# Two heads' attention scores side by side on the row halves of TensorE, in a fused attention, SwiGLU and GELU kernel

## The chip, the cores and the metric

The kernel runs on one core of a Trainium2 chip. The metric is the device time of one launch in microseconds (us), as a median over runs. A profile is one more execution, recorded by the hardware profiler.

The engines in the profile are TensorE (PE, with its weight loads as PEld), VectorE (DVE), ScalarE (ACT), GpSimd (POOL), and SyncE (SP), which here only issues DMAs.

## The reference, cut to what matters

Causal attention with an additive bias from a cumulative sum, then a gated layer with SiLU, then a layer with a sigmoid GELU. Only the attention is touched by the change:

```python
batch, n_heads, seq, head_dim = (4, 8, 576, 64)
scores = scale * np.matmul(q, k.transpose(0, 1, 3, 2))     # scale = 1/8
cum = np.cumsum(np.maximum(s, 0.0), axis=-1)
bias = -(cum[:, :, :, None] - cum[:, :, None, :])
scores = np.where(causal, -1000000000.0, scores + np.minimum(bias, 0.0))
attn = softmax(scores)                                     # with 1e-09 added to the sum
out = np.matmul(attn, v)
```

Per row of the scores the term in cum of the query is a constant and falls out of the softmax, so that the kernel only adds cum of the key to each column of the scores.

## The kernel before, in words

There are 32 heads (4 batches of 8), each of 576 positions and 64 features. A head's scores are made in five units, one PSUM bank each. A unit is one or two products of 128 queries by 64 to 448 keys (only keys that the causal mask leaves): 192 and 64 columns in unit 0, then 320, 448, 288 and 288, 1600 columns in all. After each unit DVE adds the mask, finds the row maximum and moves the scores to SBUF (the "reduction", a tensor_tensor_reduce), ACT takes the exponential and sums it, POOL divides by the sum, PE transposes the blocks (15 of 128 by 128 per head) through PSUM, ACT or DVE moves these to SBUF, and PE multiplies them with V. This last product takes two heads at once, each on one half of the array's columns (`tile_position=(0, r0)`); the trace shows its instructions as 128*64.

Scores come in two kinds. Heads 0 to 13 (`QF`) are plain: one float32 product over 128 rows, of which 64 hold the features, one the sum cum (against a row of ones), and the rest zeros. A float32 product is two matmul instructions in the trace, two passes. Heads 14 to 31 are split: q and k are rounded to float32r (one pass per product), and the remainders are kept. Product A holds on 128 rows high q with high k and low q with high k; product B holds high q with low k and two rows of cum (high and low part). To bring the halves to these rows, six DMAs per head copy 64-row pieces from SBUF to SBUF (QA, KA, QB, KB), on SP's queue, and one brings the two rows of cum from a DRAM copy.

The gated layer's first chunks (six tiles of 256 tokens, "gate products", three float32r matmuls for each weight block) are mixed into the attention on PE, as soon as all heads of a batch are done and normalised. After them PE runs one long chain for the rest of the two layers. PE's banks: scores have banks 0, 1 and 5, and bank 7 too for the first eight heads.

The order on each engine is written out at build time: `op` records each operation with a cost and a due time, and a planner (`plan`) lists them by those. The tables HD, FD, WD and TA hold due times. PE starts with idle matmuls of 512 columns (`IDLE`).

The names the change touches: `setup`, `prep_f32` and `prep` (loading q and k, rounding, copies), `scores` (the products), the tables of `PRM`, and the tiles QA, QB, KA, KB, CH and CL, which go, and QH, QL, KH, KL and KC, which come.

Of the kernel before, what the change touches and what calls it, by code (L numbers as in the profile page):

```python
# [10 lines left out]
F32 = mybir.dt.float32  # L11
F32R = mybir.dt.float32r
# [13 lines left out]
    "G0": 2, "NWS": 18, "NWO": 6,  # L26
    "QF": set(range(14)),
    "TIN": [(t * 256, 256) for t in range(6)],
    "PPB": 5, "PTB": 12, "XHB": 7, "HHB": 5,
    "VIRT": 290816,  # L30
    "SLOTS": {
        "s1": ["QB0 QB1 KB0 KB1", "B11 HH4"], "s2": ["QA0 QA1 KA0 KA1", "T1 HH5"], "s3": ["QS0 QS1 KS0 KS1", "B22 HH6"],
        "s4": ["mask", "wb"], "s5": ["SQ SQT", "SG0 SG1 V1"], "s6": ["PA0", "w9 HH0"], "s7": ["PA1", "w10 HH1"], "s8": ["PA2", "w11 HH2"],
        "si": ["PA3", "w12 HH3"], "s9": ["VS0 VS1", "M50 M51 ws"], "sb": ["PT8 PT9 PT10 PT11", "w17 HH7"], "sj": ["RE2"], "sk": ["PA4", "w6 w8"], "sl": ["w7"],
        "sc": ["SR ZR", "XH0 XH1 XH2 XH3 XH4 XH5 XH6", "MK0 MK1", "T4 w15 w16"], "sd": ["CH CL", "FH0 FH1 FH2 FH3 FH4", "B21 w13"],
        "se": ["TH0 TH1 YO", "RE0 RE1"], "sf": ["PT0 PT1 PT2", "T2"], "sg": ["PT3 PT4 PT5", "T3"], "sh": ["PT6 PT7", "w14"],
# [5 lines left out]
           (2, (8, 9)), (1, (8, 9)), (0, (8, 9)), (0, (10, 11)), (1, (10, 11)), (2, (10, 11))],  # L42
    "HD": [670.77, 588.34, 73.32, 458.6, 475.65, 350.07, 348.25, 166.97, 662.46, 625.73, 332.76, 668.93, 675.31, 193.33, 235.56, 182.94],
    "FD": [(345.51, 238.7), (69.98, 668.25), (157.32, 491.46), (669.89, 325.47), (576.97, 170.35), (699.43, 534.64)],
    "WD": [305.24, 350.84, 668.02, 164.56, 585.28, 462.76],
    "TA": 696.46, "REB": 3, "EARLY": False, "MAG": "AV", "PASS": 0, "ISSUE": 0.6, "IDLE": 7, "PEN": {}, "PVC": (0.86, 2.25),
}
# [3 lines left out]
def attention_then_swiglu_then_gelu(ctx: ExitStack, tc, qT, kT, vp, s, w1, w2, gT, out):  # L51
# [8 lines left out]
    G0 = PRM["G0"]  # L60
    QF = PRM["QF"]
    TIN = PRM["TIN"]
# [19 lines left out]
    y_d = dram.tile([P, KT, NT], F32, tag="y_d", name="y_d")  # L82
    c_d = dram.tile([HB, S], F32, tag="c_d", name="c_d")
    ch_d = dram.tile([HB, 2, S], F32, tag="ch_d", name="ch_d")
    pc_d = {
# [10 lines left out]
    wa, wm = own("wa", [512]), own("wm", [512])  # L96
    small = own("small", [128])
    small_at = [0]

    def few(n):  # L100
# [4 lines left out]
    inv_f, g_sb = few(2), few(KT)  # L105
    MX, SU, RC = [few(6) for _ in range(NB)], [few(5) for _ in range(NB)], [few(5) for _ in range(NB)]
    RY = [few(5) for _ in range(2)]

    SHAPE = {
        "Q": [S], "K": [S], "mask": [S], "SQ": [S], "VS": [5, 2 * D], "SR": [S], "ZR": [S], "CH": [S], "CL": [S], "PA": [1920], "PT": [512],  # L110
        "XH": [2, TS], "TH": [TS], "FH": [2, TS], "YO": [2, TS], "w": [2, 512], "wb": [512], "ws": [512],
        "MK": [2, 2, H2], "HH": [2, H2], "M5": [H2], "SG": [H2], "V1": [H2], "RE": [H2], **{nm: [2, 2, H2] for nm in NAMES},
    }
    ROUND = ("CH", "CL", "QA", "QB", "KA", "KB", "XH", "FH", "w", "HH", *NAMES)

# [48 lines left out]

    QS, KS, QB, KB, QA, KA, VS, TH = (get(x, 2) for x in ("QS", "KS", "QB", "KB", "QA", "KA", "VS", "TH"))
    mask, SQ, SQT, YO = (get(x) for x in ("mask", "SQ", "SQT", "YO"))
# [141 lines left out]
    def op(eng, fn, cost=None, r=None, w=None, due=None, chain=False, dma=False, g=None, after=()):  # L308
# [10 lines left out]
        if w is None:  # L319
            for name, kw in rec.calls:  # L320
                for k, x in kw.items():
                    if isap(x):
                        (wr if k in OUTS else rd).update(cells(x))
                if dma:
                    n = size(kw["out"])
                    for x in kw["out"].shape:
                        n *= x
                    o["byts"] += n
        else:
            for x in w:  # L330
                wr.update(cells(x))
            for x in r or ():
                rd.update(cells(x))
# [108 lines left out]
    def setup():  # L442
# [3 lines left out]
        op("V", lambda e: e.memset(PA[2][:, 0:512], 1.0))  # L446
        for _ in range(PRM["IDLE"]):
            op("T", lambda e: e.matmul(PB[6], PA[2][:, 0:P], PA[2][:, 0:512], start=True, stop=True), due=0.0)
        for i in range(2):
            op("G", lambda e, i=i: e.memset(KS[i][64:P, :], 0.0))  # L450
            op("G", lambda e, i=i: e.memset(QS[i][64:P, :], 1.0))
        sraw, zero, ch, cl = (get(x)[0:HB, :] for x in ("SR", "ZR", "CH", "CL"))
        cum = SQ[0:HB, :]
        dma(sraw, s)
        for h in range(2):
            prep_f32(h)
        op("V", lambda e: e.memset(zero, 0.0))
        op("V", lambda e: e.tensor_scalar(out=sraw, in0=sraw, scalar1=0.0, scalar2=8.0, op0=ALU.max, op1=ALU.mult))
        op("V", lambda e: e.tensor_tensor_scan(out=cum, data0=zero, data1=sraw, initial=0.0, op0=ALU.add, op1=ALU.add))
        for h in range(2):  # L460
            dma(KS[h][64:65, :], SQ[h:h + 1, :], eng="A", cost=0.6)
        dma(c_d, cum, eng="A", cost=0.6)
        for i in range(NB):
            op("G", lambda e, i=i: e.memset(SU[i], 1.0))
        for t in PA:
# [7 lines left out]
           cost=0.3)  # L473
        op("G", lambda e: make_identity(nc, ident), cost=0.5, w=[ident])
        rnd("V", ch, cum, cost=0.74)
        dma(ch_d[:, 0, :], ch.bitcast(F32))
        sub(cl, cum, ch, eng="V")
        dma(ch_d[:, 1, :], cl.bitcast(F32))
        for i in range(2):
            op("G", lambda e, i=i: e.memset(QB[i][64:P, :].bitcast(F32), 1.0))  # L480
            op("G", lambda e, i=i: e.memset(KB[i][64:P, :].bitcast(F32), 0.0))
        for i in range(2):
            op("V", lambda e, i=i: e.memset(VS[i][64:P, 4, :], 0.0))
        dma(g_sb, gT)

    def prep_f32(h):
        b_, hh = divmod(h, H)
        dma(QS[h % 2][0:64, :], qT[b_, hh])
        dma(KS[h % 2][0:64, :], kT[b_, hh])
        if h > 1:  # L490
            dma(KS[h % 2][64:65, :], c_d[h:h + 1, :])

    def prep(h):
        b_, hh = divmod(h, H)
        i = h % 2
        if h % 2 == 0:
            v = VS[h // 2 % 2]
            dma(v[:, 0:4, :], vp[b_, hh // 2, 0:4 * P, :].rearrange("(k p) d -> p k d", p=P))
            dma(v[0:64, 4, :], vp[b_, hh // 2, 4 * P:S, :])
        if h in QF:  # L500
            if h > 1:
                prep_f32(h)
        else:
            if i == 0:
                for t, part, src in ((QS[0], QS[1], qT), (KS[0], KS[1], kT)):
                    dma(t, src[b_, hh:hh + 2].rearrange("h d s -> (h d) s"))
                    rnd(PRM["RQ"], part.bitcast(F32R), t)
                    sub(t.bitcast(F32R), t, part)
            r0 = 64 * i
            (ql, qh), (kl, kh) = ([t[r0:r0 + 64, :] for t in x] for x in (QS, KS))  # L510
            for t, c0, x in ((QA, 0, qh), (KA, 0, kh), (KA, 64, kh), (QA, 64, ql), (QB, 0, qh), (KB, 0, kl)):
                dma(t[i][c0:c0 + 64, :].bitcast(F32), x)
            dma(KB[i][64:66, :].bitcast(F32), ch_d[h])

# [5 lines left out]
    def scores(h, u):  # L520
        ps = bank(h, "s", 5 * h + u)
        blks = {0: [(1, 0, 0, 192), (0, 192, 0, 64)], 1: [(2, 0, 0, 320)], 2: [(3, 0, 0, 448)],
                3: [(4, 0, 0, 288)], 4: [(4, 0, 288, 288)]}[u]
        i = h % 2

        def fn(e):
            for qb, c0, k0, n in blks:
                q0 = Q0[qb]
                o = ps[:, c0:c0 + n]
                if h in QF:  # L530
                    e.matmul(o, QS[i][:, q0:q0 + P], KS[i][:, k0:k0 + n], start=True, stop=True)
                else:
                    e.matmul(o, QA[i][:, q0:q0 + P], KA[i][:, k0:k0 + n], start=True, stop=False)
                    e.matmul(o, QB[i][:, q0:q0 + P], KB[i][:, k0:k0 + n], start=False, stop=True)

        first_score.append(op("T", fn)["i"])
        mx = MX[h % NB]
# [238 lines left out]
    for h in range(HB):  # L776
        prep(h)
        for u in range(5):
            scores(h, u)
        if h == 0:  # L780
            first_weights()
        recip(h)
        for qb in range(5):
            norm(h, qb)
        for t in range(4):
            transp(h, t)
        b_, hh = divmod(h, H)
        if hh % 2:
            for piece in range(2):
                pv(h - 1, piece, PRM["HD"][h // 2])  # L790
        if hh % 2:
            rms_sq(b_, hh // 2)
        if hh == H - 1:
            rms(b_)
            for j, (t0, n) in enumerate(TIN):
                if (t0 + n - 1) // S == b_:
                    fa_tile(j, fill_due)
# [322 lines left out]
    n = 0  # L1120
# [335 lines left out]
```

## Time and profile before

| what | value |
|---|---|
| median of 3 runs | 1005.71 us (1004.41 to 1006.68) |
| the profiled execution | 1005.69 us, its span 1003.9 us |
| PE busy | 991.6 us, 99% of the span |
| DVE, ACT, POOL busy | 65%, 56%, 28% |
| granted TensorE clock | 1.000 of full speed |

The attention with the gate products mixed in lasts from the start to about 262 us; from there PE runs the long chain of the two layers, which the change does not touch. PE's busy share is made of matmuls whose ends are modelled and overlap, so for PE the start times say more: the start of one group of matmuls to the start of the next is what the group took from PE's time. A row of the timeline groups neighbours by the first one's shape, so "128x192 x4" may hold two matmuls of 192 columns and two of 64.

### The profile page before, as it was taken

Reading aid. Unit: us, or ns where it says so; the run is one execution under the profiler, and the core shown is the slowest. Engines: PE = TensorE matmul, PEld = TensorE weight load, DVE = VectorE, ACT = ScalarE, POOL = GpSimd, SP = SyncE. Lnnn points to the kernel's source line nnn. Section 1 sums busy time; section 2 is a strip of 40 time slices with the busy share of each in tenths; the row PEclk is TensorE's granted clock in tenths of the full one; section 3 lists DMA queues with packets and bytes.
Section 4 is the critical chain, followed back from the end, with each engine's and each line's share of the span. In section 5 each row is a group of like instructions: output and inputs, shape, how many; then the busy total and the mean of one; then the engine's idle time right before and its main releaser. Section 6 shows DMA issues by size and latency. Waiting matters only on the chain. (4 is left out here: it accounts for less than half of the span.)

```text
span 1003.9 us, 16588 instructions
## 1 busy us (share of the span) xinstructions
PE 991.6 (99%) x5890; PEld 912.1 (91%) x5890; DVE 654.1 (65%) x1528; ACT 559.6 (56%) x1290; POOL 281.8 (28%) x387
## 2 busy tenths in 40 slices
PE   8999989999999999999999999999999999999998
PEld 5778878988899999999999999999889998899987
DVE  6788776767978887545866858874653565353323
ACT  6888976767676555334444436775644463353322
POOL 6665653443333223002321303232320231020000
PEclk9999999999999999999999999999999999999999
DMA  4436885762776763661484576653275045405541
GB/s 143 129 117 171 224 220 158 182 167 61 275 250 245 279 255 100 247 219 43 143 320 166 215 287 242 276 196 138 91 297 220 23 154 241 191 1 193 203 170 63
DMA packets 63186, 183.61 MB, mean 183 GB/s; under 512 B 7120, under 2 KB 24016, under 8 KB 63104
## 3 DMA queue, kind: packets, MB, share of 16 engines
q1 hardware_dynamic: 62992, 182.49, 53.1%
q8 instruction: 46, 0.75, 0.3%
q14 instruction: 36, 0.29, 0.1%
q10 hardware_dynamic: 112, 0.08, 0.0%
HBM read 122.35 MB, written 44.26 MB: 166 GB/s over the span
## 5 line engine op out<-in xcount | busy, mean ns | idle before, releaser
L205 ACT ACTIVATE s<-b 128x384 f32<-128x384 f32 (+1 forms) x267 | 127.7, 489 | 144.6 <-PE b L205 79.5
L205 DVE TENSOR_TENSOR xT<-b,xT 128x384 f32<-128x384 f32 (+1 forms) x158 | 92.5, 599 | 88.7 <-PE b L205 87.0
L205 ACT ACTIVATE b<-b 128x384 f32<-128x384 f32 x125 | 58.2, 478 | 107.6 <-DVE b L205 71.8
L205 PE MATMUL b<-s 128*128 128x288 f32 (+6 forms) x476 | 113.1, 367 | 3.4 <-DMA s<-s 1.7
L205 POOL TENSOR_TENSOR wa<-wa,st 128x512 int32<-128x512 int32 x50 | 65.3, 1306 | 178.2 <-DVE wa L205 83.7
L205 DVE TENSOR_TENSOR s<-b,s 128x384 fp32r<-128x384 f32 (+1 forms) x121 | 66.4, 554 | 69.5 <-ACT s L205 65.2
L205 PE MATMUL b<-s,w 128*128 128x384 f32 x540 | 107.0, 335 | 0.4 <-DVE s L205 0.2
L205 PEld LDWEIGHTS b<-s,w 128*128 128x128 f32 x540 | 94.9, 188 | 1.5 <-DVE s L205 1.0
L205 PEld LDWEIGHTS b<-s 128*128 128x128 f32 x476 | 75.5, 191 | 17.9 <-issue 6.6
L205 DVE TENSOR_TENSOR b<-b,s 128x384 f32<-128x384 f32 x82 | 46.1, 563 | 51.3 <-PE b L205 42.8
L205 POOL TENSOR_SCALAR wm<-wm 128x512 f32<-128x512 f32 x68 | 41.8, 615 | 120.2 <-ACT wm L205 42.2
L205 PE MATMUL b<-sc,w 128*128 128x256 f32 (+1 forms) x396 | 68.0, 305 | 0.0
L205 ACT ACTIVATE s<-s,small 128x448 f32<-128x448 f32 (+4 forms) x100 | 55.2, 554 | 21.3 <-DVE small L205 20.7
L205 POOL TENSOR_SCALAR s<-s,small 128x576 f32<-128x576 f32 (+4 forms) x100 | 52.1, 540 | 27.7 <-PE b L205 14.6
L205 PE MATMUL b<-sd,w 128*128 128x384 f32 (+1 forms) x312 | 58.3, 315 | 0.8 <-ACT se L205 0.8
L205 PEld LDWEIGHTS b<-sc,w 128*128 128x128 f32 x396 | 57.2, 190 | 1.6 <-issue 0.5
L205 ACT ACTIVATE st<-st 128x512 int32<-128x512 uint32 x68 | 45.6, 671 | 19.3 <-DMA st<-in_w_dram 19.3
L205 PE MATMUL b<-s,s 128*128 128x384 f32 (+1 forms) x252 | 54.9, 346 | 0.0
L205 PE MATMUL b<-w,s 128*128 128x512 f32 x189 | 51.1, 391 | 0.0
L205 PE MATMUL b<-s,sk 128*128 128x384 f32 x246 | 50.8, 335 | 0.0
L205 PEld LDWEIGHTS b<-sd,w 128*128 128x128 f32 x312 | 49.3, 189 | 1.2 <-ACT se L205 1.0
L205 PE MATMUL b<-s,sc 128*128 128x384 f32 x228 | 47.2, 334 | 0.0
(261 smaller groups left out, 2348.8 us busy)
## 6 DMA issues: line engine op xcount, KB each, us to landing
st<-in_w_dram SPq DMA_DIRECT2D x68, 512.0 KB, 3.5
s<-s SPq DMA_DIRECT2D x108, 144.0 KB, 2.7
xT<-y_d SPq DMA_DIRECT2D x3, 1536.0 KB, 7.9
s<-pc11B SPq DMA_DIRECT2D x6, 768.0 KB
s<-pc21B SPq DMA_DIRECT2D x6, 768.0 KB, 6.6
out_dram<-xT SPq DMA_DIRECT2D x18, 256.0 KB, 2.4
s<-in_vp_dram SPq DMA_DIRECT2D x16, 256.0 KB, 3.2
y_d<-se SPq DMA_DIRECT2D x12, 256.0 KB, 3.3
```

The source lines that it names most:

```text
L205: return lambda *args, **kw: f(*[real(x) for x in args], **{k: real(x) for k, x in kw.items()})
```

## The change: heads in pairs, one on each half of the rows

A unit of scores now makes both heads of a pair. Head 0 of the pair lies on rows 0 to 63, head 1 on rows 64 to 127 of the same tiles, as one DMA brings them. Each product is issued twice, once with `tile_position=(0, 0)` and once with `(64, 0)`, into two banks. Pairs 0 to 3 (`QP`) are plain: one float32 product over 64 rows. The other twelve pairs are split, as three float32r products (high by high, high by low, low by high). In both kinds one more float32r product adds cum: the constant tile KC holds high and low parts of all heads' sums on 32 rows each, and a column of zeros with two ones, broadcast to 128 columns, is the stationary operand that picks the head's two rows. No copies within SBUF are left, nor the DRAM copies of cum. q and k of a pair, which lie side by side, are rounded in one operation of 1152 columns and the remainder taken in another. The tables of due times are new, and there are six idle matmuls in place of seven.

```diff
-    "QF": set(range(14)),
+    "QP": set(range(4)),
...
-    "TA": 696.46, "REB": 3, ..., "IDLE": 7, "PEN": {}, "PVC": (0.86, 2.25),
+    "TA": 501.91, "REB": 3, ..., "INNER": 1.7, "IDLE": 6, "PEN": {}, "PVC": (1.0, 2.25), "SCC": (0.23, 0.13),
...
-        for i in range(2):
-            op("G", lambda e, i=i: e.memset(KS[i][64:P, :], 0.0))
-            op("G", lambda e, i=i: e.memset(QS[i][64:P, :], 1.0))
...
-        for h in range(2):
-            dma(KS[h][64:65, :], SQ[h:h + 1, :], eng="A", cost=0.6)
-        dma(c_d, cum, eng="A", cost=0.6)
+        rnd("AV", KC[:, 0:S], SQ)
+        for r in (HB, 3 * HB):
+            sub(KC[r:r + HB, 0:S], SQ[r:r + HB, :], KC[r:r + HB, 0:S])
+        for r, c in ((0, 0), (64, 65)):
+            x, y = (ident[r:r + 64, z:z + HB - 1:2] for z in (c, c + HB))
+            tt(KC[r:r + 64, S:S + HB // 2], x, y, ALU.add)
...
-            for t, c0, x in ((QA, 0, qh), (KA, 0, kh), (KA, 64, kh), (QA, 64, ql), (QB, 0, qh), (KB, 0, kl)):
-                dma(t[i][c0:c0 + 64, :].bitcast(F32), x)
-            dma(KB[i][64:66, :].bitcast(F32), ch_d[h])
+        if h // 2 not in QP:
+            raw, hi, lo = wide(KS[i], 2), wide(KH[i], 2).bitcast(F32R), wide(KL[i], 2).bitcast(F32R)
+            rnd(PRM["RQ"], hi, raw)
+            sub(lo, raw, hi)
...
     def scores(h, u):
-        ps = bank(h, "s", 5 * h + u)
+        i = h // 2 % 2
+        pss = [bank(h, "s", 10 * (h // 2) + 2 * u + j) for j in range(2)]
...
+        pairs = [(QS, KS)] if plain else [(QH, KH), (QH, KL), (QL, KH)]
         def fn(e):
-            for qb, c0, k0, n in blks:
-                if h in QF:
-                    e.matmul(o, QS[i][:, q0:q0 + P], KS[i][:, k0:k0 + n], start=True, stop=True)
-                else:
-                    e.matmul(o, QA[i][:, q0:q0 + P], KA[i][:, k0:k0 + n], start=True, stop=False)
-                    e.matmul(o, QB[i][:, q0:q0 + P], KB[i][:, k0:k0 + n], start=False, stop=True)
+            for x, (qt, kt) in enumerate(pairs):
+                for y, (qb, c0, k0, w) in enumerate(blks):
+                    for j, ps in enumerate(pss):
+                        r = slice(64 * j, 64 * j + 64)
+                        e.matmul(ps[:, c0:c0 + w], qt[i][r, Q0[qb]:Q0[qb] + P], kt[i][r, k0:k0 + w],
+                                 start=x == 0 and y == 0, stop=False, skip_group_check=True, tile_position=(64 * j, 0))
+            for y, (qb, c0, k0, w) in enumerate(blks):
+                for j, ps in enumerate(pss):
+                    r = slice(64 * j, 64 * j + 64)
+                    e.matmul(ps[:, c0:c0 + w], KC[r, S + h // 2:S + h // 2 + 1].to_broadcast([64, P]), KC[r, k0:k0 + w],
+                             start=False, stop=y == len(blks) - 1, skip_group_check=True, tile_position=(64 * j, 0))
```

The order of PE at the start, before the change, from the second head's unit 2 on. Banks 0, 1, 5 and 7 hold scores, s3 holds q and k, s6 and s8 hold a head's attention weights, and ident marks a transpose:

```order
L205 MATMUL b7_73<-s3_0_137 128x448
L205 MATMUL b5_71<-s3_0_137 128x320
L205 MATMUL b0_66<-s3_0_137 128x288
L205 MATMUL b1_67<-s3_0_137 128x288
L205 MATMUL b2_68<-ident_120,s6_0_184 128x128 x4
```

The same place after the change, from unit 2 of the second pair (sj is the constant tile KC):

```order
L208 MATMUL b5_71<-s3_0_135 128x448
L208 MATMUL b7_73<-s3_0_135 128x448
L208 MATMUL b5_71<-sj_0_149 128x448
L208 MATMUL b7_73<-sj_0_149 128x448
L208 MATMUL b0_66<-s3_0_135 128x288
L208 MATMUL b1_67<-s3_0_135 128x288
L208 MATMUL b0_66<-sj_0_149 128x288
L208 MATMUL b1_67<-sj_0_149 128x288
L208 MATMUL b2_68<-ident_118,s6_0_163 128x128 x4
```

Ahead of the first transposes there were ten units of one head (heads 0 and 1); now there are nine units of two heads (pair 0 and four fifths of pair 1).

In the middle, before the change, a unit of a split head (s2 and s1 hold the A and the B operands) between transposes:

```order
L205 MATMUL b3_69<-ident_120,sk_0_210 128x128 x4
L205 MATMUL b5_71<-s2_0_978 128x288
L205 MATMUL b5_71<-s1_0_216 128x288
L205 MATMUL b2_68<-ident_120,sk_0_210 128x128 x4
```

And the last unit of the last pair after the change (s2 holds the high and low parts; w marks gate products or their second layer). Between its first two rows and its last two stand two more such pairs of rows:

```order
L208 MATMUL b2_68<-ident_118,si_0_194 128x128 x4
L208 MATMUL b7_73<-sd_0_1363,w5_129 128x256 x3
L208 MATMUL b5_71<-s2_0_657 128x288
L208 MATMUL b0_66<-s2_0_657 128x288
...
L208 MATMUL b5_71<-sj_0_149 128x288
L208 MATMUL b0_66<-sj_0_149 128x288
L208 MATMUL b6_72<-sc_1_970,w0_124 128x256 x3
```

Two matmuls of one head over 128 rows have become eight of two heads over 64 rows each. What lies on either side (transposes and gate products) still runs over 128 rows and 128 columns. Over the whole order the scores form 70 stretches: 64 are entered from work on the whole array (39 from transposes, 20 from gate products, 5 from the normalisation) and 6 from a product with V; 64 are left to work on the whole array (41 to transposes, 21 to gate products, 2 to the normalisation) and 6 to a product with V.

## Rows read from the trace of the kernel before

**Rows 1.** Busy time by stretch: us, then busy (and count) of each engine, clock, DMA.

```profile
25.00:75.00 50.00, 50.00 (x353) 37.56 (x352) 39.53 (x154) 42.47 (x127) 33.55 (x55) 1.00 0.40 123
75.00:125.00 50.00, 50.00 (x406) 42.49 (x405) 40.17 (x145) 43.50 (x135) 29.29 (x48) 1.00 0.75 197
175.00:225.00 50.00, 50.00 (x426) 45.75 (x422) 36.81 (x135) 34.81 (x103) 21.00 (x39) 1.00 0.67 177
```

**Rows 2.** PE's waits in 0 to 262 us: total, times, longest.

```profile
PE b L205 <- DMA s<-s: 1.7, 1, 1.7
PE b L205 <- POOL s L205: 1.7, 1, 1.7
PE b L205 <- ACT se L205: 0.8, 1, 0.8
PE b L205 <- ACT sb L205: 0.7, 1, 0.7
```

**Rows 3.** PE's timeline, 16 to 20 us: start, us, instructions [wait before].

```profile
16.69 0.66 PE L205 MATMUL b<-ident,s 128*128 128x128 f32 x4 [1.68 <-POOL s L205]
17.18 2.97 PE L205 MATMUL b<-s 128*128 128x192 f32 x12
19.99 0.71 PE L205 MATMUL b<-ident,s 128*128 128x128 f32 x5
```

**Rows 4.** PE's timeline, split units: starts of a unit and of what follows.

```profile
172.34 0.53 PE L205 MATMUL b<-s 128*128 128x192 f32 x4
172.70 0.36 PE L205 MATMUL b<-sd,w 128*128 128x256 f32 x1
...
194.38 0.52 PE L205 MATMUL b<-sd,w 128*128 128x256 f32 x3
194.74 0.57 PE L205 MATMUL b<-s 128*128 128x448 f32 x2
195.15 0.52 PE L205 MATMUL b<-sd,w 128*128 128x256 f32 x3
195.50 0.43 PE L205 MATMUL b<-s 128*128 128x288 f32 x2
195.77 0.49 PE L205 MATMUL b<-ident,sk 128*128 128x128 f32 x3
```

**Rows 5.** PE's timeline, 31 to 34 us, around a product with V.

```profile
31.43 1.04 PE L205 MATMUL b<-ident,s 128*128 128x128 f32 x8
32.40 0.43 PE L205 MATMUL b<-sf,s 128*64 128x256 f32 x1
32.41 0.43 PE L205 MATMUL b<-sg,s 128*64 128x256 f32 x1
...
33.20 0.76 PE L205 MATMUL b<-s 128*128 128x192 f32 x4
```

**Rows 6.** PE's timeline, 41 us: one step of 320 columns to the next.

```profile
41.25 0.43 PE L205 MATMUL b<-sb,s 128*64 128x320 f32 x1
41.26 0.43 PE L205 MATMUL b<-sf,s 128*64 128x320 f32 x1
41.52 0.43 PE L205 MATMUL b<-sb,s 128*64 128x320 f32 x1
```

**Rows 7.** PE's timeline, 204 us: three transposes of 64 and 128 rows.

```profile
204.30 0.72 PE L205 MATMUL b<-ident,small 64*128 64x64 f32 x3
204.95 0.63 PE L205 MATMUL b<-sd,w 128*128 128x256 f32 x3
205.41 0.60 PE L205 MATMUL b<-ident,s 128*128 128x128 f32 x4
```

**Rows 8.** DVE groups, 0 to 262 us: reductions, and a remainder.

```profile
L205 DVE CUSTOM_DVE_ANT_0 s<-b,s 128x448 f32<-128x448 f32 (+4 forms) x100 | 39.2, 424 | 10.9 <-PE b L205 10.7
L205 DVE TENSOR_TENSOR s<-s 128x576 fp32r<-128x576 f32 x12 | 9.0, 762 | 0.7 <-ACT s L205 0.6
L205 DVE TENSOR_SCALAR s<-s 128x576 fp32r<-128x576 f32 x13 | 6.0, 465 | 0.4 <-DMA s<-ch_d 0.4
```

**Rows 9.** DMA issues of the whole run.

```profile
s<-s SPq DMA_DIRECT2D x108, 144.0 KB, 2.7
```

## What the change was predicted to do

> **What bounds the kernel now.** I read the busy shares by stretch first. In the attention PE is busy all of the time in three stretches of 50 us, where DVE has 37 to 40 us of work, ACT 35 to 44 and POOL 21 to 34 [rows 1]. The clock is granted in full in each. Next I read what PE waits for: four waits of 0.7 us or more in 262 us, 4.9 us together [rows 2]. So PE's own work sets the end of this stage; the chain after it is untouched and dense. The change is then priced by PE's time alone: what each kind of work takes from one start to the next, since ends are modelled.
>
> **Scores, now.** A plain head (12 matmuls) starts at 17.18 and the transposes behind it at 19.99: 2.81 us [rows 3]. Of this 2.67 are columns (1600, two passes, two cycles each at 2.4 GHz). Units of a split head take 0.36 (192 and 64 columns, A and B), 0.41 (448) and 0.27 (288) [rows 4]; I put 320 columns between these, at 0.30. A split head is 0.36 + 0.30 + 0.41 + 2 x 0.27 = 1.61 us. All scores: 14 x 2.81 + 18 x 1.61 = 68.3 us.
>
> **Scores, after.** No row shows two products on row halves. The nearest are the products with V, two heads on the column halves: the two start 0.01 us apart, and the next step of 320 columns comes 0.27 us later, which is the two passes of one of them [rows 6]. So two halves do run in the time of one there, their weight loads included. I take the same for row halves. A plain pair is then one head's 2.81 and one float32r product for the sums, half of 1.61: 3.6 us. A split pair is four products, 4 x 0.805 = 3.2 us, and 0.1 more in unit 0, where a step of 64 columns cannot be shorter than the weight load of 128 columns (0.10, below). In all 4 x 3.65 + 12 x 3.35 = 54.8 us, 13.5 less than before. Who looks closer sees where it comes from: the four plain pairs save 2.0 each, the three pairs that turn from plain to split 2.3 each, and the nine pairs that were split already save nothing (3.35 for 3.22): two products per head before, four per two heads now. The bounds: with no overhead beyond columns 45.3 us, 23 less than before; with the halves one after the other 110 us, 41 more.
>
> **What it adds: changes of the array's shape.** The product with V is the one kind of work that often leaves the whole array, and its rows show a price. Eight transposes (0.86 by their columns) start at 31.43 and the product only at 32.40: 0.11 lost on the way in. Its 384 columns of two passes take 0.64; the next scores start 0.80 after its start: 0.16 lost, the load of the first weights and the way out [rows 5]. That could be a matter of column halves. But three small transposes over 64, 128 and 64 rows stand in the trace, at 128 columns each way of the weights: 0.65 us for 0.21 of columns [rows 7], so each change between 64 and 128 rows costs some 0.145, a drain of 0.095 and 0.05 of load that nothing hides. And the three gate products behind them take 0.46 where three such take 0.36 elsewhere [rows 7, 4]: their first load of 128 columns is bare too, 0.10. A load of a score's operand is of that kind.
>
> So a stretch of scores on row halves pays 0.095 + 0.10 on entry, and on leaving 0.095 + 0.05 before transposes or 0.20 before gate products. The order has 64 entries from the whole array, 43 exits to transposes and the normalisation and 21 to gate products: 64 x 0.195 + 43 x 0.145 + 21 x 0.195 = 12.5 + 6.2 + 4.1 = 22.8 us. Products with V are as many as before and pay as before. The bounds: the drain alone, 128 x 0.095 = 12.2 us, if loads slip under it; nothing, if float32r products change shape freely, for which no row speaks; and no row shows more than 0.20 at a change.
>
> The Trainium skill (TensorEngine Tiling (Array Packing), Key Properties) says that a change of tiling mode drains TensorE, and names no price. The 0.095 agrees with that, and the row adds the bare load, of which the rule says nothing; by the drain alone the total of this document would be near 1002.
>
> **The rest.** Copies within SBUF go (108 of 144 KB on SP's queue [rows 9]), and with them the one PE wait on such a copy: -1.7 us [rows 2]. Behind the copies SP's queue held loads of weights, which PE never waits for by name, so no more is counted. What is late next at that place is the rounding of the pair, an operation of DVE, ACT or POOL.
>
> Rounding and remainders: twelve pairs for nine, one operation for two. By DVE's rows two of each are 2 x (0.465 + 0.762) = 2.5 us per pair of heads [rows 8], so three more pairs add at most 7.4 us over three engines. PE's work covers it; the tightest is ACT with 43.5 of 50 us [rows 1]. If all of it fell on one engine that PE waits for, it would cost those 7.4.
>
> The start: one idle matmul less is two passes of 512 columns, -0.86. But DVE now reduces both heads in turns, so head 0 is done at the eleventh reduction, not the sixth, five times 0.424 later [rows 8], and the transposes that now start at 16.69, after a wait of 1.68 for POOL [rows 3], would start at 16.69 + 2.1 - 0.86 = 17.9. PE's nine units of a pair are over at 15.3 (9.4, from 16.69 - 1.68 - 2 x 2.81, less 0.86, plus 0.2 and 9 x 0.73), so it waits 2.6: 0.9 more than now. Together zero.
>
> Banks: from the fifth pair on a unit takes two of three banks, so the next one waits on PE until the first half is reduced (0.42 us), with all of PE's queue behind it. The order puts transposes or gate products between most units: 80 units stand in 70 stretches, so ten follow one another directly, most of them in the first pairs with four banks. I count nothing; at most 10 x 0.42 = 4.2.
>
> The end of the stage: more gate products are left behind the last product with V, which covers the wait of 0.8 for ACT [rows 2]: -0.8.
>
> **Sum.** -13.5 + 22.8 - 1.7 + 0 - 0.8 = +6.8 us. On the profiled execution (1005.69, of which 1003.9 are the span), which is the median of the runs, that makes 1012.5.
>
> **Rivals.** First, faster: the halves run nearer to their columns, since one half's pauses are filled by the other, and the loads at a change slip under the drain. For it: in rows 6 a step of two halves has no more than 0.003 over its columns. Against it: those are float32 passes; a float32r unit of 288 columns takes 0.27 for 0.24 [rows 4], and the bare load is seen at every kind of work. With half of the two gaps to the bounds (-18 and +17.5) the sum is -3.0, 1002.7; with all of them -23 + 12.2 - 2.5 = -13.3, 992.4. It is at 997 in the middle.
>
> Second, the change does not do what it says: weight loads or streams of the two row halves take turns. If each step paid its load, 24 steps of a split pair and 18 of a plain one would add 12 x 2.4 + 4 x 1.8 = 36 us: 1049; if the streams themselves took turns, 1012.5 + 55 = 1067. Against it stand rows 6, where two loads and two streams share a step. The Trainium skill (TensorE: Matmul & The Clock Gate, Part 3, The mechanism) has a rule for the first: a weight load overlaps a running matmul only if its row group differs. By it half 0's next load would wait for half 0's running product, and the 1049 follow. The trace disagrees on the whole array, where all loads have the same rows: gate products keep 0.12 a piece [rows 4] though each has a load of 0.10, so I give it little.
>
> Third, slower by waits: DVE's reductions, now in pairs, set the pace, as PE needs two banks at once. It decides from the point where DVE is over 0.4 us late at a unit. DVE has 20% to spare [rows 1], and PE itself gets slower; if every second of the 60 split units waited one reduction, 30 x 0.42 = 12.7 us more, 1025.
>
> **Chances.** The forecast 0.52, faster by denser halves 0.30, loads or streams in turns 0.08, paced by DVE 0.10. A measurement of this kernel tells 0.2%, 2 us, from no change. Slower by more than that: 0.52 + 0.08 + 0.10, less some of the forecast's own lower edge, 0.64; the denser halves give 0.26 faster; 0.10 lies between. The forecast's own range is 1007 to 1019. To hold 8 in 10 the range takes in most of the denser halves (from 994) and the paced case (to 1028).
>
> **What would show it.** In the profile after: the two matmuls of a step start 0.01 apart, and a split unit of 288 columns takes some 0.54 (0.27 if it were one product per head, 1.1 if in turns). Between the last gate product or transpose and the first score 0.2 us are missing, and as much on the way out. The first transposes start near 18. The stage's end moves from 262 to about 269, and the long chain behind it keeps its 742 us. I am wrong if the changes of shape cost less than 0.1 a side, if a step stays clearly under its columns plus 0.013, or if PE has waits of over 5 us in the stage.

## The result, and the profile after

The changed kernel takes 1019.79 us (median of four runs, 1018.54 to 1020.15), the kernel before 1005.06 beside it: the ratio is 1.014, its 95% interval 1.0125 to 1.016. The forecast was 1012.5, slower by 6.8; it is slower by 14.7. So the sign and the main mechanism came out as forecast, and two further losses of about 6 us each had been put at nothing. The time lies just above the forecast's own range of 1007 to 1019, and inside the wide one of 994 to 1028.

The page of the profile after, its first lines:

```profile
span 1018.2 us, 16887 instructions
PE 1006.3 (99%) x6224; PEld 913.9 (90%) x6224; DVE 647.6 (64%) x1507; ACT 565.7 (56%) x1292; POOL 295.7 (29%) x389
PEclk8999999999999999999999999999999999999999
```

PE is as full as before, on a span 14.3 us longer. To place these I mark the two matmuls `b<-w` of 512 columns that open the long chain, and its last group of three. In PE's timeline before:

```profile
268.25 0.63 PE L205 MATMUL b<-w 128*128 128x512 f32 x2
...
999.30 0.84 PE L205 MATMUL b<-sk,s 128*128 128x512 f32 x3
```

And after:

```profile
276.52 0.62 PE L208 MATMUL b<-w 128*128 128x512 f32 x2
...
1013.67 0.85 PE L208 MATMUL b<-sk,s 128*128 128x512 f32 x3
```

The chain opens 8.27 us later, and from its opening to its last group it takes 737.15 us where it took 731.05: another 6.10, though it holds the same matmuls in the same order. (The first two expectations below count to the end of the span, 741.7 and 735.6; the later ones count to the last matmul itself, 0.46 later than here: 737.6 and 731.5.)

What answers to [rows 2] in the stage before the chain, PE's waits in 0 to 285 us:

```profile
PE b L208 <- DMA s<-in_qT_dram: 2.3, 1, 2.3
PE b L208 <- DVE small L208: 1.8, 2, 1.5
PE b L208 <- DVE sj L208: 1.1, 2, 0.8
PE b L208 <- POOL s L208: 0.7, 2, 0.4
```

These are the first four of nine kinds; all nine come to 7.9 us. The wait for a copy within SBUF is gone. New are waits for q and for the constant tile sj, both in the first 14 us. The 1.5 for `small` stands ahead of PE's first matmul; the kernel before has the like of it, 1.4, which [rows 2] leave out, so it does not enter the difference. What answers to [rows 3], PE's start:

```profile
10.64 0.80 PE L208 MATMUL b<-s 64*128 64x192 f32 x8 [2.32 <-DMA s<-in_qT_dram]
12.26 0.53 PE L208 MATMUL b<-sj 64*128 64x192 f32 x1 [0.82 <-DVE sj L208]
13.05 0.52 PE L208 MATMUL b<-sj 64*128 64x192 f32 x2 [0.26 <-DVE sj L208]
...
23.29 0.66 PE L208 MATMUL b<-ident,s 128*128 128x128 f32 x4 [0.28 <-POOL s L208]
```

The first transposes start at 23.29, where 16.69 was and near 18 was forecast. And what answers to [rows 4], the middle:

```profile
183.45 0.60 PE L208 MATMUL b<-sd,w 128*128 128x256 f32 x3
183.98 0.71 PE L208 MATMUL b<-s 64*128 64x320 f32 x6
184.52 0.31 PE L208 MATMUL b<-sj 64*128 64x320 f32 x2
184.76 0.62 PE L208 MATMUL b<-sd,w 128*128 128x256 f32 x3
```

Here one reads the price of a change of shape. Six matmuls on row halves are three steps of 320 columns, and a step within a stretch takes 0.145 us (median of all such steps): 0.44. They take 0.54, 0.10 more, which is the bare first load of the forecast. The step of the sums takes 0.24, 0.09 more than 0.145, which is the forecast's drain ahead of the gate products.

### The profile page after: what moved, and what is told of

Read it like the earlier page. It is cut to its first block, busy times and chain, and to the rows that moved or that the text cites. A ratio compares the mean times of both kernels' runs of the same rounds, so it can differ in the third digit from the quotient of the medians.

```text
span 1018.2 us, 16887 instructions
## 1 busy us (share of the span) xinstructions
PE 1006.3 (99%) x6224; PEld 913.9 (90%) x6224; DVE 647.6 (64%) x1507; ACT 565.7 (56%) x1292; POOL 295.7 (29%) x389
## 4 chain that ended last, share of the span: by engine, by line
PE 95%; DVE 3%; DMA 1%; ACT 1%; POOL 1%; issue 0%; DVEq 0%
PE b L208 95%; DMA sc<-in_s_dram 1%; DVE s L208 1%; DVE xT L208 1%; POOL s L208 1%; ACT s L208 0%; DVE sd L208 0%; DVE sj L208 0%; DVE b L208 0%; DVE sf L208 0%; ACT sf L208 0%; ACT sg L208 0%; DVE sb L208 0%; ACT L208 0%; DVE sc L208 0%
## 5 line engine op out<-in xcount | busy, mean ns | idle before, releaser
L208 PE MATMUL b<-s 64*128 64x288 f32 (+6 forms) x618 | 92.6, 360 | 4.2 <-DMA s<-in_qT_dram 2.3
L208 PEld LDWEIGHTS b<-s 64*128 64x128 f32 (+1 forms) x618 | 58.3, 190 | 21.5 <-issue 11.4
L208 PE MATMUL b<-sc,w 128*128 128x256 f32 (+1 forms) x396 | 70.1, 309 | 0.0
L208 ACT ACTIVATE s<-s,small 128x192 f32<-128x192 f32 (+4 forms) x100 | 55.1, 553 | 15.3 <-DVE small L208 14.9
L208 POOL TENSOR_SCALAR s<-s,small 128x192 f32<-128x192 f32 (+4 forms) x100 | 52.9, 549 | 20.6 <-DVE small L208 10.6
L208 DVE CUSTOM_DVE_ANT_0 s<-b,s 128x192 f32<-128x192 f32 (+4 forms) x100 | 40.1, 426 | 15.2 <-PE b L208 14.3
```

The costliest lines, as they stand in the source:

```text
L208: return lambda *args, **kw: f(*[real(x) for x in args], **{k: real(x) for k, x in kw.items()})
```

## Experiments on the long chain: where its 6.1 us come from

Neither PE's order nor that of another engine differs in the chain. What differs is where buffers stand in SBUF: the tile `small` is shorter, so that everything behind it begins 32 bytes past a multiple of 64, and buffers get their place in the order of first use, which is another one.

**A shift of everything.** In after_align `small` moves behind all buffers, which puts the rest on multiples of 64; in before_off32 the kernel before gets the shift.

```diff
+    tail = ctx.enter_context(tc.tile_pool(name="tail", bufs=1))   # after_align
...
-    small = own("small", [72])
+    small = tail.tile([P, 72], F32, tag="small", name="small")
-    small = own("small", [128])                       # before_off32
+    small = own("small", [104])
```

> The changed kernel with one edit: the small tile (288 bytes per partition) moved to the end of SBUF, so that every other tile starts at a multiple of 64 bytes again, as before the change, and not 32 bytes past one. The orders of all engines stay as in the changed kernel. Theory A (the offset makes TensorE's reads slower): the chain behind the attention, which takes 741.7 us in the profile after and 735.6 before from the same two matmuls to the end, goes back to 735.6 to 736.5; total about 1014, 5.5 to 6.5 us less. Rival (another cause, as the transfers of the chain or the clock): the chain stays at 741 to 742 and the total at 1019 to 1020.

> The kernel before the change with one edit: the small tile is 416 bytes per partition in place of 512, so that all tiles behind it start 32 bytes past a multiple of 64. Orders unchanged. Theory A: the chain behind the attention goes from 735.6 to 741 to 742 us, the total to about 1011. Rival: no difference, 1005 to 1006.

Measured: after_align 1019.74 (ratio 1.015, 1.0135 to 1.0165), its chain 737.2; before_off32 1006.49 (1.0014, 1.0004 to 1.0024), its chain 730.96. The theory fell: a shift common to all buffers behind `small` does nothing to the chain.

**The order of the buffers.** Two kernels give every buffer its first tile at the start, in the other kernel's order. Nothing moves on any engine.

```diff
+    for slot in "s8 sc s3 s9 s4 s5 sd s6 s7 si sk s1 sf sg sh sb s2 se sl sj".split():   # after_place: order of before
...
+        tiles[slot, 0] = slots.tile(...)
...
-    small = own("small", [128])                                                         # before_place: order of after
+    small = own("small", [96])
...
+    WIDE["sj"] = 2240
...
+    for slot in "s8 sc s3 s4 sj s9 s6 s7 s5 si sk sf sg sh sb s1 s2 se sd sl".split():
...
+        tiles[slot, 0] = slots.tile(...)
```

> The changed kernel, its buffers in SBUF laid out in the order of the kernel before; every engine's order is unchanged. Theory (the long chain is slower because its operands lie elsewhere relative to one another): the chain goes back from 737.6 to some 731.5, the total from 1019.8 to 1013.7. Rival (what slows the chain is not the place of its operands): chain within 1 of 737.6, total within 1.5 of 1019.8.

> The kernel before, its buffers in SBUF laid out in the order of the changed kernel; every engine's order is unchanged. Theory (place of the operands): the chain goes from 731.5 to some 737.6, the total from 1005.0 to 1011. Rival: chain within 1 of 731.5, total within 1.5 of 1005.

Measured: after_place 1014.34 (1.0101, 1.0079 to 1.0123), before_place 1012.24 (1.0076, 1.0059 to 1.0092). Two groups of the chain by shape (busy, mean ns of one), before:

```profile
L205 PE MATMUL b<-s,w 128*128 128x384 f32 x540 | 107.0, 335 | 0.4 <-DVE s L205 0.2
L205 PE MATMUL b<-w,s 128*128 128x512 f32 x189 | 51.1, 391 | 0.0
```

after:

```profile
L208 PE MATMUL b<-s,w 128*128 128x384 f32 x540 | 107.4, 337 | 0.2
L208 PE MATMUL b<-w,s 128*128 128x512 f32 x189 | 51.6, 394 | 0.0
```

after_place:

```profile
L208 PE MATMUL b<-s,w 128*128 128x384 f32 x540 | 107.2, 335 | 0.4 <-DVE s L208 0.2
L208 PE MATMUL b<-w,s 128*128 128x512 f32 x189 | 51.1, 391 | 0.0
```

before_place:

```profile
L206 PE MATMUL b<-s,w 128*128 128x384 f32 x539 | 107.4, 337 | 0.2
L206 PE MATMUL b<-w,s 128*128 128x512 f32 x189 | 51.4, 393 | 0.0
```

The loss goes and comes with the places, in both directions: the chain takes 731.91 in after_place and 736.78 in before_place. (The shorter `small` of before_place shifts all buffers behind it alike.) From one start to the next, a mean over the chain without gaps over 0.25 us, a matmul of 384 columns takes 173.7 ns in the kernel before and 174.7 in the changed one, one of 512 takes 228.3 and 231.1. That is 0.6 and 1.2%, at a granted clock of 1.00 in both, and over the chain's some 3060 and 865 matmuls 5.5 of the 6.1 us; the rest is in the longer gaps.

**Order, or an offset.** In the kernel before every buffer has a multiple of 256 bytes a row. In the changed kernel sj holds the constant tile with its 16 unit columns, 592 elements or 2368 bytes, and stands fifth: all buffers behind it are 64 bytes off, modulo 256, against those ahead. (In before_place, by its 2240 bytes, it is 192.) after_uc gives the unit columns a tile of their own (sj, now 2304 bytes, also comes three places later, by its first use); before_pad128 lengthens one buffer of the kernel before by 128 bytes.

```diff
-        ... "KC": [S + HB // 2], ...                   # after_uc
+        ... "KC": [S], ...
...
+    UC = own("uc", [HB // 2], F32R)
...
+    WIDE["s4"] += 128                                  # before_pad128
```

> The changed kernel with the unit columns in a small tile of their own, so that the constant tile's buffer has 2304 bytes a row, a multiple of 256 like all other buffers, and no longer 2368; buffers stay in the changed kernel's order, the engines' work is the same. Theory (buffers behind that one stand 64 bytes off, modulo 256, against those ahead of it, and this slows the chain): chain 731.5 to 732.5, total near 1014. Rival (the order of the buffers in SBUF is what counts): chain 737.6, total 1019.8.

> The kernel before with one buffer (mask, wb) 128 bytes a row longer, so that the buffers behind it stand 128 bytes off against those ahead, modulo 256; every engine's order is unchanged. Theory (offsets count modulo 256, so 128 costs as 64 and 192 did): chain 735 to 738 instead of 731.5, total 1009 to 1012. Rival (they count modulo 128, and 64 was the bad one): chain within 1 of 731.5, total within 1.5 of 1005.

Measured: after_uc 1014.93 (1.009, 1.0069 to 1.0111), before_pad128 1011.61 (1.0059, 1.0035 to 1.0082). Their timelines, after_uc:

```profile
276.73 0.63 PE L209 MATMUL b<-w 128*128 128x512 f32 x2
...
1008.59 0.84 PE L209 MATMUL b<-sk,s 128*128 128x512 f32 x3
```

before_pad128:

```profile
268.57 0.62 PE L206 MATMUL b<-w 128*128 128x512 f32 x2
...
1006.98 0.86 PE L206 MATMUL b<-sk,s 128*128 128x512 f32 x3
```

The chains take 731.86 and 738.41. So with the changed kernel's order otherwise kept, the 64 bytes make the loss, and 128 bytes put into the kernel before cost it 7.4 us. The order by itself costs nothing that these runs show. Offsets of 64, 128 and 192 have all been seen to cost, multiples of 256 not (in after_uc and before, buffers of 9 times 256 bytes stand in the middle). What in the memory does this stays open; I didn't find a rule that tells which pair of operands is slow.

## Experiments on the start

**s sooner, and no half clock.** In the changed kernel one DMA with repeated rows brings s, 8.3 us from issue (0.74) to landing (9.07). after_s4 takes four DMAs of 32 rows. And between 12 and 18 us the changed kernel's clock is granted at half level, behind 2.3 us in which PE waited; after_idle12 has idle matmuls until the scores begin.

```diff
-        dma(sraw, bass.AP(s.tensor, s.offset, [(0, P // HB), (S, HB), (1, S)]), due=0.0)   # after_s4
+        for r in range(0, P, HB):
+            dma(sraw[r:r + HB, :], s, due=-90.0)
...
-    ... "IDLE": 6, ...                                                                     # after_idle12
+    ... "IDLE": 12, ...
```

> The changed kernel with one edit: s is loaded by four DMAs of 32 rows each, not by one DMA that repeats it four times (which landed at 9.07 us, issued at 0.74). Theory B (the late sums hold the start): the scan starts at about 6, the first reduction at 10 to 10.5 in place of 13.74, the first transposes at about 20 in place of 23.3, total 3 to 4 us less, about 1016. Rival (the start is paced by the reductions of two heads in turns, whatever the load): the first transposes come less than 1.5 us earlier and the total stays within 1.5 us of 1019.8.

> The changed kernel with twelve idle matmuls in place of six: PE is busy until about 13.5 us, has no 2.3 us wait at the start, and should keep its full clock (in the profile after, 6.8 us at half the clock follow the wait). Scores start 3 us later. Theory C (the half clock is what the start loses): 3 us or more less, 1016 or below. Theory B (the late sums and DVE set the first transposes, the clock little): within 1.5 us of 1019.8, and the first transposes between 22.5 and 24.

Measured: after_s4 1019.36 (1.0146, 1.013 to 1.0163), first transposes at 22.28; after_idle12 1020.29 (1.016, 1.0143 to 1.0177), clock 1.00 throughout, first transposes at 23.12. Neither helps by itself, but neither settles its question. The four DMAs brought s no sooner: DVE could start on it at 8.35, and with the one DMA at 8.38 to 9.08 in five profiles. And the full clock of after_idle12 is paid for with a later start of the scores. Its first reduction and its first transposes:

```profile
14.54 0.36 DVE L208 CUSTOM_DVE_ANT_0 s<-b,s 128x192 f32<-128x192 f32 x1 [2.24 <-PE b L208]
```

```profile
23.12 0.66 PE L208 MATMUL b<-ident,s 128*128 128x128 f32 x4 [0.28 <-POOL s L208]
```

DVE's timeline in the changed kernel, from the landing of s on:

```profile
9.08 0.46 DVE L208 TENSOR_SCALAR sc<-sc 128x576 f32<-128x576 f32 x1 [6.37 <-DMA sc<-in_s_dram]
9.58 1.36 DVE L208 TENSOR_TENSOR_SCAN s<-sc 128x576 f32<-128x576 f32 x1
10.97 0.46 DVE L208 TENSOR_SCALAR sj<-s 128x576 fp32r<-128x576 f32 x1
11.46 1.53 DVE L208 TENSOR_TENSOR sj<-s,sj 32x576 fp32r<-32x576 f32 x2
13.74 0.36 DVE L208 CUSTOM_DVE_ANT_0 s<-b,s 128x192 f32<-128x192 f32 x1 [0.75 <-POOL small L208]
...
16.87 0.62 DVE L208 CUSTOM_DVE_ANT_0 s<-b,s 128x448 f32<-128x448 f32 x1 [0.95 <-PE b L208]
```

Scan, rounding and remainders take 3.9 us behind s, and only then can any unit be finished by its sums. The first reduction starts at 13.74; before it was at 10.05. From there to the first transposes it takes 9.55 us (13.74 to 23.29), where after_idle12 at full clock takes 8.58 (14.54 to 23.12): at half level DVE waits for PE, 0.95 us at 16.87 alone. So the half clock costs about 1 us here, and after_idle12 gives 0.8 of it back by its later first reduction.

**Without that path.** after_nosum makes the constant tile from zeros, and so leaves the sums out, with s by four DMAs as in after_s4 and all buffers where the changed kernel has them.

```diff
...
-        op("V", lambda e: e.tensor_tensor_scan(out=SQ, data0=zero, data1=sraw, ...))
-        rnd("AV", KC[:, 0:S], SQ)
+        rnd("AV", KC[:, 0:S], zero)
...
```

> The changed kernel with s loaded by four DMAs and the constant tile made from zeros at once, so that no score waits for the scan (the sums are left out of the scores); same buffers, same places. Theory (the start is late because the first reductions wait for qT and for the constant tile, and because both heads are reduced in turns): first reduction near 11 instead of 13.74, first transposes near 20.3 instead of 23.3, total 3 less, near 1016.8. Rival (the turns or the half clock alone hold the start): first transposes stay beyond 22, total within 1.5 of 1019.8.

Measured: 1015.0 (1.0101, 1.0075 to 1.0128). In its timelines the first reduction and the first transposes, and the opening of the chain:

```profile
9.35 0.36 DVE L208 CUSTOM_DVE_ANT_0 s<-b,s 128x192 f32<-128x192 f32 x1 [4.36 <-PE b L208]
```

```profile
17.95 0.66 PE L208 MATMUL b<-ident,s 128*128 128x128 f32 x4 [0.29 <-POOL s L208]
...
271.20 0.62 PE L208 MATMUL b<-w 128*128 128x512 f32 x2
```

The chain opens 5.3 us sooner than in the changed kernel, more than expected, and the first transposes stand where the forecast had them (17.9). From the first reduction to there it takes 8.60, against 6.64 before the change (10.05 to 16.69): 1.96 more for the 2.1 of the forecast. So the forecast had the turns of both heads right, and what it left out is the path by the constant tile, and q, which lands behind s. Of the 5.3 us, 4.4 are the earlier first reduction; 0.95 is the half clock that follows PE's waits in the changed kernel, while here the clock is granted in full throughout. Without all this the stage is still 2.95 longer than before (271.20 to 268.25).

## Experiments on the price of a change of shape

The kernel before gets one extra float32 matmul of 64 columns ahead of each of 64 groups of transposes, over 64 rows in the one and over 128 in the other.

```diff
+            if h >= 16:
+                e.matmul(ps[:, ...], ident[0:64, :], ident[0:64, 0:64], start=True, stop=True)      # before_visit64
+                e.matmul(ps[:, ...], ident[0:128, :], ident[0:128, 0:64], start=True, stop=True)    # before_visit128
...
```

> The kernel before with one added matmul of 64 columns over 64 rows ahead of each of the 64 groups of transposes of heads 16 to 31 (the output doesn't use it). Theory (leaving the whole array and coming back costs 0.195 + 0.145): 64 x 0.34 = 22 us more than the control over 128 rows, at least 18. Rival (a change of shape is cheap, the loss in the changed kernel is elsewhere): under 6 us more than the control.

> Control to the one over 64 rows: the same added matmul of 64 columns, over all 128 rows, at the same 64 places. Both theories: only its own time, two passes of some 0.06 to 0.11, 8 to 14 us over the kernel before.

Measured: 1038.04 (1.0344, 1.0293 to 1.0394) and 1015.42 (1.0106, 1.0091 to 1.0121), 22.6 us apart. Three of the four executions over 64 rows show a mean granted clock of 0.987 to 0.996, and the profiled one has the half level from 134 to 161 us; the one at full clock took 1034.28, which is 18.9 over the control, or 0.295 for each visit. The timelines, in stretches at full clock, of before_visit64:

```profile
222.23 0.42 PE L205 MATMUL b<-s 128*128 128x288 f32 x2
222.58 0.43 PE L205 MATMUL b<-ident 64*128 64x64 f32 x2
222.94 0.66 PE L205 MATMUL b<-ident,sk 128*128 128x128 f32 x4
```

and of before_visit128:

```profile
199.38 0.43 PE L205 MATMUL b<-s 128*128 128x288 f32 x2
199.65 0.33 PE L205 MATMUL b<-ident 128*128 128x64 f32 x2
199.81 0.61 PE L205 MATMUL b<-ident,sk 128*128 128x128 f32 x4
```

From the score to the transposes it is 0.71 against 0.43: 0.28 for going to 64 rows and back, with the same columns. The theory held; the price in the forecast (0.195 in, 0.145 out) was some 15% high for this kind of visit.

## A version meant to beat both

Split heads are the cheaper ones for PE, so the kernel before was given more of them.

```diff
-    "QF": set(range(14)),
+    "QF": set(range(8)),
```

> The kernel before with 8 plain heads instead of 14, so six heads more are split (float32r); its plan is made anew by the same rules. Theory (PE bounds the stage, and a split head takes 1.61 for 2.81 of a plain one): 6 x 1.2 = 7.2 us less, near 998. Rival (the copies within SBUF and the roundings that split heads need come too late early in the stage, and PE waits for them): gain under 2 us, or a loss.

Measured: 1012.28 (1.0067, 1.0041 to 1.0094), slower. PE's waits in 0 to 280 us, the longest kinds:

```profile
PE b L205 <- ACT sf L205: 1.9, 3, 1.0
PE b L205 <- DMA s<-ch_d: 1.9, 2, 1.1
PE b L205 <- POOL s L205: 1.8, 1, 1.8
PE b L205 <- POOL sk L205: 1.5, 1, 1.5
```

The rival held in that there is no gain and PE waits more: all kinds listed in that view come to 13.2 us, against 7.9 in the kernel before. But these 5.3 us do not account for everything: the chain opens 4.25 later (272.50 for 268.25), so PE's other time fell by only 1.0 and not by 7.2. Why is not shown. The due times were made for 14 plain heads, so this doesn't show that no plan with eight could win.

## Why the prediction was right, and where it was not

For the terms, each kind of matmul got its median time to the next start as its pace; what lies above it, up to 0.25 us, is counted by the kinds of the two neighbours, and longer gaps as waits. In us:

| term | forecast | measured |
|---|---|---|
| scores themselves | 68.3 to 54.8: -13.5 | 73.2 to 54.7: -18.5 |
| changes of shape, products with V apart | +22.8 | +20.3 |
| start, to the first transposes | 0 | +5.3 |
| long chain | 0 | +6.1 |
| the rest: PE's other waits, end of the stage, and what is left to the sum | -2.5 | +1.2 |
| sum | +6.8 | +14.4 |

What the forecast was about, denser scores against changes of shape and the rest, makes 3.0 us of this, 2.95 by after_nosum. So the sign was forecast for the right reason, but most of the 14.7 came by the two terms that were put at nothing, and that the time still fell near the forecast's own range is in part luck.

**Two halves side by side: right.** The two matmuls of a step start 3 to 6 ns apart, and the pace of all scores comes to 54.7 us, for 54.8 (in after_nosum, whose start does not blur it; 55.7 in the changed kernel). The rival by which loads or streams take turns (36 or 55 us more) is out: within a stretch a step of 320 columns takes 0.145 us, 0.012 over its columns, with no load showing. With it goes, here, the time that would follow from the rule of the Trainium skill (TensorE: Matmul & The Clock Gate, Part 3, The mechanism) which the prediction cites. Loads do show in unit 0, where columns are few. PE's weight loads there:

```profile
49.78 0.74 PEld L208 LDWEIGHTS b<-s 64*128 64x128 f32 x12 [0.17 <-issue]
50.44 0.30 PEld L208 LDWEIGHTS b<-sj 64*128 64x128 f32 x4
```

Twelve loads in six pairs take 0.66 us, 0.11 a pair, so that a product of 192 and 64 columns takes two such, 0.22, for 0.107 of columns. The two halves load side by side, and the 0.1 more that the forecast gave unit 0 for this was near: four products at 0.22, not at half of 0.36, make 0.16 more.

**Changes of shape: right, and the cause of the loss that was meant.** By neighbours: drains on the way in 5.4, the first step's bare load 5.3, drains on the way out 5.4, bare first loads of the transposes and gate products behind 4.1; 20.3 together. A drain is 0.09 to 0.10 each way, as [rows 7] had it.

**Scores before: the term came out larger.** I priced a split head at 1.61 from single units [rows 4]. Summed over all 18 they take 34.1, 1.90 each; the plain ones 39.1, as forecast. By this count denser work on halves was worth 5 us more than I gave it. But part of the 5 us is only a matter of which neighbour is charged. The units priced in [rows 4] stand behind gate products; the next one stands between transposes:

```profile
195.77 0.60 PE L205 MATMUL b<-ident,sk 128*128 128x128 f32 x4
196.12 0.51 PE L205 MATMUL b<-s 128*128 128x288 f32 x2
196.47 0.60 PE L205 MATMUL b<-ident,sk 128*128 128x128 f32 x4
```

This unit takes 0.35 instead of 0.27, but the four transposes ahead of it take 0.35 where four at their median of 0.109 would take 0.44. And in the order of the kernel before scores stood next to a product with V 24 times, after it 12 times; the price of the other changes to and from V has moved to transposes and gate products. How much of the 5 us is real is not separated here; the part that is not stands in the table's last row with the other sign.

**"Together zero", for the start: failed.** I worked out the eleven reductions correctly and let them begin where the old ones did. That step needed a look at what the new sums wait for: a landing at 9.07 and 3.9 us of DVE behind it, and the half clock behind PE's waits. By the forecast's own sign, PE waits of over 5 us in the stage, this part was wrong: they are 7.9 us, as many as before the change, but 5.2 of them now lie ahead of the first transposes.

**"The chain after it is untouched": failed.** Its instructions are; the places of its operands are not. No row of the trace before could have priced it, but the buffer's new length, S + HB // 2 columns, stood in the diff.

**Waits, and reductions setting the pace:** from the first transposes to the chain all PE waits of the profile come to 4.8 us before and 2.4 after, so that the forecast's -2.5 was right for the waits, and this rival did not decide.

## What to carry to other kernels

Price a change of the array's shape at some 0.3 us for going and coming back, and count such changes in the order before halving columns by packing: here twenty microseconds of changes ate a gain of at most eighteen. When an edit changes a buffer's length, look where every operand of the untouched matmuls ends up; here buffers at multiples of 256 bytes a row against one another kept the chain at its best. And a term that must be there before the first result can leave PE (here the sums) is part of the start's chain, even if it is small.

## What the runs showed of the hardware that was not expected

- The offset between operands' places, modulo 256 bytes, changes the pace of matmuls of 384 and 512 columns by 0.6 to 1.7% (228.3 to 231.1 ns at 64 bytes, 232.3 at 128). The pattern over the single matmuls of 512 columns repeats from run to run (correlation 0.97 and more between kernels of one layout) and has next to nothing in common between layouts (0.2 at most).
- Some 6 us at half clock in the start cost about 1 us (9.55 us from the first reduction to the first transposes, 8.58 and 8.60 at full clock). With 64 short visits to 64 rows three of four executions were below full clock, the profiled one at half level from 134 to 161 us without a wait of PE ahead of it; the control over 128 rows stayed at full clock. What brought this is not shown.
- One DMA that reads the same 32 rows four times took 7.6 to 8.3 us for 295 KB in five profiles, in the company of the first loads; four plain DMAs of 32 rows had all landed no sooner.
